# New estimates in a kernel builder's clock: program blocks, centring pieces, and the order that follows

## The chip, the cores and the metric

The kernel runs on one core of a Trainium2 chip. The metric is device time in microseconds; the time of a kernel is the median of several executions. One further execution is recorded by the hardware profiler, and all stages, gaps and rows below come from it. TensorE is called PE, VectorE DVE, ScalarE ACT, GpSimd POOL, and SyncE SP.

## The reference

Eight batches (B), eight heads (H), 576 positions (S), head size 64 (D): Nyström attention with 32 landmarks, and then a layer norm with two dense layers and a residual on the joined heads.

```python
q_lm = q.reshape(B, H, m, S // m, D).mean(axis=3)      # m = 32
k_lm = k.reshape(B, H, m, S // m, D).mean(axis=3)
A, Bm, C = sm(q, k_lm), sm(q_lm, k_lm), sm(q_lm, k)    # softmax of scaled products
Z = Bm.T / (norm1(Bm) * norminf(Bm) + 1e-06)
for _ in range(6):
    Z = 2 * Z - Z @ Bm @ Z
x = A @ Z @ C @ v                                      # heads joined: 8 x 576 x 512
xn = (x - mu) / np.sqrt(var + 1e-06) * g_ln
out = x + np.maximum(xn @ w_ch1, 0.0) @ w_ch2          # 512 -> 2048 -> 512
```

## The kernel before, in words

**The work.** Attention is done for batch 0, then 1, 2, the pair (3,4), the pair (5,6), and 7. A unit is four heads; a batch has two. `Coming` (L716) brings a set: `load` puts 576 KB of k, q or v into a ring of six staging tiles (SP's queue), `cast` (L775) makes fp16 of it on POOL (`nat`, or `natv` for v) and for some units also adds up the segments there (`asum`, `s`), `turn` and `turn_sums` or `add_up` transpose and sum on DVE (`xT`, `sT`, `part`), `spread` (L847) lays the landmarks out by a matmul and a copy on ACT (`lm`). `attention2` (L907) then has, in this order: the landmark scores, their softmax on DVE and `scores_k` (L864, exponentials `ec` on ACT, transposes `ecT` on DVE), `gram_of` (L663), six `iterate` (L683: a PE product, then one DVE operation that writes `st`), and beside them `scores_q` (L885, `ea`), the product with V in parts (`product`, L953, `pscv`), the divisors (`psd` on PE, two `lns` operations on ACT) and `normalize` (L509), which multiplies `ea` by `lns` on POOL. Last come `pszt`, `pszc`, the `zcbd` tiles (DVE), and `rows_of` (L697), which makes the attention's output block by block (`xblk`).

**The dense layers.** `First` (L1127) does a batch's first layer: four `product_of_heads` (L1135, "heads": eight matmuls, two copies to `m`), and sixteen chunks (L1158) of four matmuls into `psh`, each evacuated by a relu to `hT` on ACT or on DVE. `second_layer` (L1381) does the second in blocks of 128 rows, 16 matmuls a block; from batch 4 on most of it goes as seven half-size products (`seven_products`, L1312), for which POOL mixes W2 (`mix_w2`, L1267) and DVE mixes `hT`. W1 is centred in place by eight DVE operations of 1024 columns (`center_w1`, L1120), two for each quarter of the columns, after batch 1's last `product_of_heads`.

**What sets the order.** Nothing in the order of instructions is written out by hand for the middle of the kernel. The kernel's own builder keeps a clock (`Clock`, L83): each recorded operation goes through `note` (L146), which adds an estimated duration (`took`, L124) to the engine's time and notes when its tiles are ready and free. `run` (L1509) holds four streams (attentions, first layers, batch 0's rows, second layers). Each says from what time its next piece could go; the first that could go by now is taken, in that order of preference, and where none can, the soonest. Before each choice `help_out` (L1424) places stores, loads, POOL casts, centring pieces and DVE jobs, if the engine's estimated time is near enough. The instructions keep the order of recording on each engine. So an estimate changes no operation but may change every order.

The clock also counts matmuls, for the blocks in which PE's program is fetched: a `mark` at which the next block is taken to begin (L93), `BLOCK` matmuls later the next one (L103), and `fetched`, the estimated end of the running fetch: `FETCH` ns after the mark while loads are on the wire, 3000 otherwise (L178 to L181). At a mark the clock holds PE until `fetched`; `calm` (L105) lets attention's dense pieces of some 40 to 72 matmuls ask whether a mark comes inside them.

```python
        def calm(self, n):

            return self.fetched if self.count + n + (20 if late() else 0) >= self.mark else 0.0
```

Where there is nothing to do for PE, `warm` (L463) puts a matmul on zeros.

Of the kernel before, what the change touches and what calls it, by code (L numbers as in the profile page):

```python
# [20 lines left out]
def kernel(  # L21
# [19 lines left out]
    KCH = DM // P  # L41
    MCH = HID // P
# [19 lines left out]
    def name_of(x):  # L62
        return x.tensor.name if hasattr(x, "tensor") else x.name

    parted, mixed_ = {}, set()

    def key_of(ap):

# [2 lines left out]
    def keys_of(ap):  # L71
        n = name_of(ap)
        if n not in parted:
            return [n]
        at = [ap.offset]
        for step, k in list(ap.ap)[1:]:
            if step >= parted[n]:
                at = [o + step * i for o in at for i in range(k)]
        if n in mixed_:
            return [f"{n}:{o // parted[n]}:{int(o % parted[n] >= 256)}" for o in at]  # L80
        return [f"{n}:{o // parted[n]}" for o in at]

    class Clock:  # L83
# [5 lines left out]
        def __init__(self):  # L89
            self.free = dict.fromkeys(("PE", "DVE", "Activation", "Pool", "SP"), 0.0)  # L90
            self.wrote, self.used, self.begun = {}, {}, {}
            self.small, self.lanes, self.wire = False, {}, 0.0
            self.cells, self.count, self.mark, self.fetched = [], 0, 100, 0.0  # L93

        def share(self, span=3400.0):

# [3 lines left out]
        def now(self):  # L100
            return max([self.free["PE"]] + list(self.lanes.values()))

        BLOCK, FETCH = 127, 4300  # L103

        def calm(self, n):  # L105

# [17 lines left out]
        def took(self, i, e, n, m):  # L124
            op = type(i).__name__
            if e == "Activation":
                return 190 + 0.79 * n
            if e == "Pool":
                if n == 1024 and name_of(i.outs[0].bass_ap) in mixed_:
                    return 2080  # L130
                if "Ptr" in op:
                    return 100 + 1.29 * n
                return 100 + 0.92 * n if "Copy" in op else 280 + 1.76 * n
            if n == 1152 and "Copy" in op:
                return 760
            if "Stats" in op:
                return 690 if m > 100 else 180
            if n >= 512 and (n == 576 or op == 'InstTensorCopy'):
                return 100 + 1.13 * n
            if n == 1024:  # L140
                return 690 if name_of(i.outs[0].bass_ap) in mixed_ else 900
            if "Transpose" in op:
                return 110 + 1.15 * n
            return 140 + 1.15 * max(n, m if "Reduce" in op else 0)

        def note(self, i):  # L146
            e = str(i.engine).rsplit(".", 1)[-1]
            outs = [a.bass_ap for a in i.outs if hasattr(a, "bass_ap")]
            ins = [a.bass_ap for a in i.ins if hasattr(a, "bass_ap")]
            size = [[k for _, k in a.ap] for a in outs + ins]  # L150
            count = []
            for dims in size:
                n = 1
                for k in dims[1:]:
                    n *= k
                count.append(n)
            reads = [n for a in ins for n in keys_of(a)]
            writes = [n for a in outs for n in keys_of(a)]
            ready = 0.0
            for n in reads:  # L160
                t, who = self.wrote.get(n, (0.0, e))
                if who != e or e != "PE":
                    ready = max(ready, t + (self.WAY if who != e else 0.0))
            for n in writes:
                for t, who in (self.wrote.get(n, (0.0, e)), self.used.get(n, (0.0, e)),
                               (self.begun.get(n, 0.0), "")):
                    if who != e:
                        ready = max(ready, t + self.WAY)
            if type(i).__name__ == "InstDMACopy":
                start = max(self.free[e], ready)  # L170
                self.free[e] = start + (580 if e == "SP" else 100)
                self.wire = max(start + 1650, self.wire) + count[0] * size[0][0] * 4 / 385.0
                done = self.wire + 600 + min(2200, 0.6 * (self.wire - start - 1650))
                start = done
            elif e == "PE":
                cols = count[0]
                self.count += 1
                if self.count >= self.mark:  # L178
                    self.mark += self.BLOCK
                    ready = max(ready, self.fetched)  # L180
                    self.fetched = max(self.now(), ready) + (self.FETCH if self.wire > self.now() else 3000)  # L181
                rows_, cols_ = tuple(i.tile_size)
                self.cells.append((self.now(), cols / 2.4 * rows_ * cols_ / 128 ** 2))
                if tuple(i.tile_size) == (128, 128):
                    if self.small:
                        self.free[e] = max(list(self.lanes.values()) + [self.free[e]]) + 100
                        self.small, self.lanes = False, {}
                    start = max(self.free[e], ready)
                    self.free[e] = start + max(cols / 2.4 + 3, 56)
                    done = self.free[e] + 160  # L190
                else:
                    if not self.small:
                        self.small, self.lanes = True, {}
                        self.free[e] += 95
                    lane = [(a, c) for a in range(i.tile_position[0], i.tile_position[0] + rows_, 32)
                            for c in range(i.tile_position[1], i.tile_position[1] + cols_, 32)]
                    start = max([self.free[e], ready] + [self.lanes.get(x, 0.0) for x in lane])
                    self.lanes.update((x, start + max(cols / 2.4, 30)) for x in lane)
                    self.free[e] = start + (8 if rows_ == 64 and cols < 128 else 4)
                    done = self.lanes[lane[0]] + 160  # L200
            else:
                start = max(self.free[e], ready)
                done = start + self.took(i, e, count[0], max(count[1:] + [0]))
                self.free[e] = done - self.OVERLAP[e]
            for n in reads:
                self.used[n] = max(self.used.get(n, (0.0, e)), (done, e))
            for n in writes:
                self.wrote[n] = max(self.wrote.get(n, (0.0, e)), (done, e))
# [160 lines left out]
    w1_16 = wpool.tile([P, KCH, HID], FP16, name="w1_16")  # L369
    w2_16 = wpool.tile([P, MCH, DM], FP16, name="w2_16")  # L370
    parted[w1_16.name] = parted[w2_16.name] = 512
    w1_src = moe_w_ch1.rearrange("(c p) f -> p c f", p=P)
    w2_src = moe_w_ch2.rearrange("(m p) d -> p m d", p=P)
    xpool = Ring(name="xpool", bufs=12)
# [137 lines left out]
    heads, ready, multiplied, cast_v = {}, set(), {0}, {0}  # L512
# [1094 lines left out]
```

## Time and profile before

| what | value |
|---|---|
| median of 3 runs | 286.38 us |
| lowest and highest | 285.69, 287.48 us |
| the profiled execution | 287.15 us |
| its span on the core | 285.4 us |
| granted PE clock, mean | 1.000 |
| PE, DVE, ACT, POOL busy | 267.0, 216.0, 162.5, 159.2 us |
| HBM read and written | 36.70 and 9.44 MB |

The span runs from the first to the last instruction; 1.75 us of the profiled execution lie around it. Busy times overlap, since the engines run side by side; what counts is the engine that ends a wait last. A timeline row has a start and a length in us, the engine, the tiles written and read, their shapes, and in brackets the idle time before it with what ended it. "issue" there means that the profile shows nothing that the engine waited for.

How the stages lie in the span, by the order of PE's matmuls and their times in the trace: batch 0's attention to 24 us, batch 1's from 43 to 54, batch 2's from 73 to 89, the pair (3,4) from 110 to 133, batch 3's first layer from 133 to 152, batch 4's from 152 to 168, the pair (5,6) from 139 to 180, batch 5's first layer from 188, batch 7's attention from 225 to 237, batch 7's first layer from 244 to 258, and second layers to the end.

### The profile page before, as it was taken

Reading aid. Unit: us, or ns where it says so; the run is one execution under the profiler, and the core shown is the slowest. Engines: PE = TensorE matmul, PEld = TensorE weight load, DVE = VectorE, ACT = ScalarE, POOL = GpSimd, SP = SyncE. Lnnn points to the kernel's source line nnn. Section 1 sums busy time; section 2 is a strip of 40 time slices with the busy share of each in tenths; the row PEclk is TensorE's granted clock in tenths of the full one; section 3 lists DMA queues with packets and bytes.
Section 4 is the critical chain, followed back from the end, with each engine's and each line's share of the span. In section 5 each row is a group of like instructions: output and inputs, shape, how many; then the busy total and the mean of one; then the engine's idle time right before and its main releaser. Section 6 shows DMA issues by size and latency. Waiting matters only on the chain.

```text
span 285.4 us, 8685 instructions
## 1 busy us (share of the span) xinstructions
PE 267.0 (94%) x3620; PEld 165.5 (58%) x3620; DVE 216.0 (76%) x480; ACT 162.5 (57%) x286; POOL 159.2 (56%) x187
## 2 busy tenths in 40 slices
PE   7887999998899899989889999999999999999994
PEld 7644554345334465434455555467876766678883
DVE  3558985999999754998798842899697299747761
ACT  2566955278633787336999866647338653672000
POOL 5377777999999999998999975610000030100000
PEclk9999999999999999999999999999999999999999
DMA  7999999987744589792830011130041004300606
GB/s 246 386 390 386 385 390 393 310 274 252 246 122 133 192 272 329 216 315 56 261 112 2 2 34 44 39 74 2 0 111 41 0 5 99 89 0 2 147 19 167
DMA packets 23375, 46.70 MB, mean 164 GB/s; under 512 B 2212, under 2 KB 2472, under 8 KB 23336
## 3 DMA queue, kind: packets, MB, share of 16 engines
q1 hardware_dynamic: 23176, 46.02, 49.9%
q8 instruction: 28, 0.46, 0.6%
q10 hardware_dynamic: 160, 0.13, 0.2%
q14 instruction: 11, 0.09, 0.1%
HBM read 36.70 MB, written 9.44 MB: 162 GB/s over the span
## 4 chain that ended last, share of the span: by engine, by line
PE 47%; POOL 18%; DVE 14%; DMA 13%; issue 4%; ACT 1%; SPq 1%; POOLq 0%; DVEq 0%; ACTq 0%
PE bank L272 31%; PE psh L272 13%; POOL natv L266 6%; DMA stg<-in_v_dram 6%; DMA wstg<-in_moe_w_ch_dram 5%; POOL asum L266 4%; POOL nat L266 4%; DVE w L266 3%; DVE xblk L266 2%; DVE xT L266 2%; DMA stg<-in_k_dram 2%; POOL ea L266 2%; DVE part L266 1%; DVE m L266 1%; DVE six L266 1%
## 5 line engine op out<-in xcount | busy, mean ns | idle before, releaser
L272 PE MATMUL bank<-w,hT 128*128 128x512 f16 (+1 forms) x528 | 108.7, 335 | 1.4 <-issue 1.4
L266 ACT ACTIVATE hT<-psh 128x576 f16<-128x576 f32 x114 | 71.3, 651 | 18.5 <-PE psh L272 16.6
L272 PE MATMUL psh<-ea,m 128*128 128x288 f16 x512 | 77.4, 286 | 3.1 <-ACT hT L266 1.3
L272 PEld LDWEIGHTS <-hT 128*128 128x128 f16 x656 | 60.6, 98 | 32.7 <-issue 7.1
L272 PEld LDWEIGHTS <-m 128*128 128x128 f16 x512 | 47.9, 97 | 24.8 <-issue 10.0
L266 DVE SCALAR_TENSOR_TENSOR xblk<-bank,rstd,xblk 128x256 f32<-128x256 f32 (+1 forms) x77 | 39.2, 541 | 24.6 <-PE bank L272 24.5
L266 POOL TENSOR_TENSOR ea<-ea,lns 128x576 f16<-128x576 f16 x14 | 18.1, 1305 | 47.9 <-ACT lns L266 47.9
L266 POOL CAST natv<-stg 64x1152 f16<-64x1152 f32 (+1 forms) x23 | 26.7, 1159 | 12.5 <-DMA stg<-in_v_dram 8.7
L266 POOL CAST nat<-stg 128x1152 f16<-128x1152 f32 x28 | 32.5, 1177 | 2.0 <-DMA stg<-in_k_dram 1.1
L266 ACT CAST m<-bank 128x512 f16<-128x512 f32 x31 | 17.5, 587 | 12.9 <-PE bank L272 12.7
L266 ACT COPY xblk<-bank 128x512 f32<-128x512 f32 (+1 forms) x32 | 17.8, 589 | 11.9 <-PE bank L272 11.8
L266 DVE BATCH_NORM_STATS2 six<-xblk 128x6 f32<-128x512 f32 x36 | 24.3, 674 | 0.3 <-ACT xblk L266 0.2
L266 DVE STREAM_TRANSPOSE xT<-nat 128x576 uint32<-128x576 uint32 x28 | 21.5, 767 | 1.1 <-POOL nat L266 0.8
L266 DVE TENSOR_REDUCE part<-xT 128x32 f16<-128x576 f16 x28 | 20.3, 743 | 0.3
L266 ACT ACTIVATE lns<-psd 128x576 f32<-128x576 f32 x16 | 10.3, 646 | 17.1 <-PE psd L272 17.1
L266 POOL TENSOR_TENSOR asum<-asum 128x256 f32<-128x256 f32 (+1 forms) x28 | 17.5, 626 | 2.2
L266 DVE CAST m<-bank 128x512 f16<-128x512 f32 x17 | 11.7, 687 | 7.6 <-PE bank L272 7.4
L266 POOL TENSOR_TENSOR asum<-nat 128x512 f32<-128x512 f16 x14 | 16.8, 1200 | 1.1
L272 PE MATMUL bank<-w2mix,hT 128*128 128x256 f16 x128 | 16.5, 273 | 0.0
L272 PE MATMUL bank<-w2mix 128*128 128x256 f16 x128 | 16.0, 273 | 0.0
L272 PE MATMUL bank<-zcbd,ea 128*128 128x256 f16 (+1 forms) x80 | 13.9, 275 | 1.5 <-DVE m L266 0.8
L272 PE MATMUL bank<-w,zt 64*32 64x512 f16 x256 | 14.2, 386 | 0.5 <-ACT less L266 0.4
(123 smaller groups left out, 341.0 us busy)
## 6 DMA issues: line engine op xcount, KB each, us to landing
stg<-in_q_dram SPq DMA_DIRECT2D x16, 576.0 KB, 6.0
stg<-in_k_dram SPq DMA_DIRECT2D x16, 576.0 KB, 5.4
stg<-in_v_dram SPq DMA_DIRECT2D x16, 576.0 KB, 6.5
out_dram<-xblk SPq DMA_DIRECT2D x70, 128.0 KB, 2.3
wstg<-in_moe_w_ch_dram SPq DMA_DIRECT2D x16, 512.0 KB, 7.0
out_dram<-xblk ACTq DMA_DIRECT2D x2, 64.0 KB, 2.3
out_dram<-xblk SPq DMA_DIRECT2D x2, 64.0 KB, 2.0
g_rows<-in_moe_g_ln_dram SPq DMA_DIRECT2D x1, 2.0 KB
```

Source lines behind the costliest of these rows:

```text
L266: return lambda *args, **kw: keep(getattr(self.engine, op)(*args, **kw))
L272: keep(nc.tensor.matmul(o, l, r, start=start, stop=stop, tile_position=(rb, cb), skip_group_check=(skip or cb != 0)))
```

## The change

Four places in the clock get other numbers, and one rule is new. The first mark is at 116 matmuls instead of 100. A fetch is taken to last 5000 ns with loads on the wire instead of 4300, and 3300 without instead of 3000. A DVE operation of 1024 columns outside the mixing of `hT` (a centring piece of W1) is taken to last 1080 ns instead of 900. And when such a piece is recorded on a part of W1, POOL's estimated time moves on by 430 ns, counted from the piece's start if POOL would be free before.

```diff
-            self.cells, self.count, self.mark, self.fetched = [], 0, 100, 0.0
+            self.cells, self.count, self.mark, self.fetched = [], 0, 116, 0.0
...
-        BLOCK, FETCH = 127, 4300
+        BLOCK, FETCH = 127, 5000
...
-                return 690 if name_of(i.outs[0].bass_ap) in mixed_ else 900
+                return 690 if name_of(i.outs[0].bass_ap) in mixed_ else 1080
...
-                    self.fetched = max(self.now(), ready) + (self.FETCH if self.wire > self.now() else 3000)
+                    self.fetched = max(self.now(), ready) + (self.FETCH if self.wire > self.now() else 3300)
...
                 self.free[e] = done - self.OVERLAP[e]
+                if e == 'DVE' and count[0] == 1024 and writes[0] in parted_w1:
+                    self.free['Pool'] = max(self.free['Pool'], start) + 430
...
     parted[w1_16.name] = parted[w2_16.name] = 512
+    parted_w1.update(f"{w1_16.name}:{i}" for i in range(KCH * MCH))
```

None of these lines issues an instruction. The built program has 3618 matmuls on PE instead of 3620 (two matmuls on zeros fewer), and the same loads, casts, products and stores in another order, beginning with batch 1's attention. On DVE and ACT one evacuation changes engine.

More of the change, by code (lines that the diff above doesn't have):

```diff
@@ L63, in name_of @@
         return x.tensor.name if hasattr(x, "tensor") else x.name
-    parted, mixed_ = {}, set()
+    parted, mixed_, parted_w1 = {}, set(), set()
     def key_of(ap):
```

## The prediction

> **What bounds the kernel now.** First the page's engine totals and slices: which engine is full, and where.
>
> ```profile
> PE 267.0 (94%) x3620; PEld 165.5 (58%) x3620; DVE 216.0 (76%) x480; ACT 162.5 (57%) x286; POOL 159.2 (56%) x187
> ...
> POOL 5377777999999999998999975610000030100000
> PEclk9999999999999999999999999999999999999999
> DMA  7999999987744589792830011130041004300606
> ```
>
> The span has to hold TensorE's work. PE has 18.4 us of idle time in it; POOL is full from about 50 to 142 us; the clock is granted throughout, so no step below is a matter of clock. Next the stages, as busy time in windows (us of the window, then PE, PEld, DVE, ACT, POOL, clock, DMA share, GB/s).
>
> ```profile
> 95.00:110.00 15.00, 13.67 (x138) 8.21 (x144) 8.32 (x17) 11.54 (x22) 14.23 (x15) 1.00 0.72 235
> 110.00:126.00 16.00, 15.42 (x444) 7.40 (x427) 14.20 (x36) 8.22 (x13) 15.00 (x19) 1.00 0.87 280
> 126.00:141.00 15.00, 12.42 (x155) 6.06 (x153) 12.61 (x25) 10.04 (x20) 13.20 (x13) 1.00 0.54 159
> 141.00:152.00 11.00, 9.89 (x85) 5.92 (x84) 10.15 (x20) 10.28 (x18) 10.30 (x14) 1.00 0.36 126
> 152.00:168.00 16.00, 16.00 (x275) 9.31 (x275) 10.47 (x27) 13.44 (x25) 16.00 (x15) 1.00 0.01 2
> 168.00:188.00 20.00, 19.85 (x333) 9.75 (x331) 13.02 (x28) 11.32 (x21) 10.34 (x10) 1.00 0.23 53
> 188.00:285.00 97.00, 93.05 (x1034) 71.19 (x1026) 69.53 (x152) 42.46 (x77) 5.01 (x4) 1.00 0.23 53
> ```
>
> From 152 us on PE is full but for the tail; an order can only win before that. So third, PE's timeline around its gaps there (start, us, tile, idle before, releaser).
>
> ```profile
> 75.98 0.19 PE L272 MATMUL bank<-st,bones 128*128 128x64 f16 x1 [1.13 <-DVE st L266]
> ...
> 99.10 0.38 PE L272 MATMUL bank<-part,spread 128*128 128x256 f16 x2 [1.33 <-DVE part L266]
> ...
> 117.93 0.32 PE L272 MATMUL psea<-xT,lm 32*32 32x288 f16 x8 [0.56 <-issue]
> ...
> 127.85 1.90 PE L272 MATMUL bank<-w,hT 128*128 128x512 f16 x8 [1.38 <-issue]
> ...
> 141.15 1.07 PE L272 MATMUL psh<-ea,m 128*128 128x288 f16 x6 [0.70 <-ACT ec L266]
> ```
>
> Two gaps wait for DVE, two for nothing the profile names, one for ACT. The two unnamed ones are waits for program. The trace's DMA records show 28 instruction packets of 16,384 bytes on queue q8; one starts at 115.74 and PE resumes 2.2 us later, one at 125.44 and PE resumes 2.4 us later; the resumed matmuls are numbers 1503 and 1759 (from 0), 256 apart, so a block is 128 matmuls and edges lie at 95+128k. After both waits the next packet starts 1.63 us on, which is the fetch's free lead: an unhindered fetch costs 1.63 + 2.2 = 3.8 us. Counting from where the sequencer asks (it runs some 28 matmuls ahead: in the long stages packets start 1.63 us after number edge-28), these two took about 7 us, with the DMA share at 0.87.
>
> Last, the queues behind those gaps.
>
> ```profile
> 70.03 5.30 DVE L266 TENSOR_TENSOR w<-w,less 128x1024 f16<-128x1024 f16 x5
> ...
> 131.54 2.61 POOL L266 TENSOR_TENSOR ea<-ea,lns 128x576 f16<-128x576 f16 x2 [1.27 <-ACT lns L266]
> ...
> 140.28 1.48 ACT L266 ACTIVATE ec<-psec 128x576 f16<-128x576 f32 x2
> 141.83 2.71 ACT L266 ACTIVATE hT<-psh 128x576 f16<-128x576 f32 x4
> ```
>
> **The change part by part.** No operation is added and only two PE fillers of 0.28 us at most go; six estimates of the builder change, and the order follows. I compared the two programs' orders engine by engine; matmul numbers are places in PE's order. Up to number 609 PE's order is the same. Then A(n) is the attention of batch n.
>
> *A(1), number 610.* The product with V is put after one more iteration and two second-layer matmuls. It waited 0.42 us for natv; POOL casts k1 ahead of both ea, filling its 0.59 us wait there and making ea 0.5 us later, which nobody needs before 57 us. Gain 0 to 0.4 at PE, counted 0, since first layer 1 that follows is paced by evacuation.
>
> *Centring.* A piece costs 0.93 us at the median, one 1.62. The old estimate 0.9 put five ahead of A(2)'s softmax, the new 1.08 puts four. Softmax's row sum starts 1.62-0.08 us earlier, the gap of 1.13 shrinks to about 0.2: gain 0.9. The piece returns behind the transposes of ec; there nine second-layer matmuls (9x0.215=1.9 us) now stand in front of the first iteration and cover it. Each later iteration still queues on DVE behind a transpose (0.77) or a sum (0.74); I give 0.2 back. Net -0.7.
>
> *The 430 ns on POOL.* It moves no work. [...] I take 0.
>
> *spread for (3,4), second half.* It moves from number 1216 to 1264, behind 48 matmuls (some 4 us). It waited for DVE's part at 99.05, which waited for POOL's sum at 98.45; PE now gets there after 101. Gain 1.3. On SP, loads of (3,4) v2, v3 and (5,6) k0, k1 now stand behind stores of blocks that DVE finishes at 82 to 95 us; casts need them at 102 to 107, so nothing is late.
>
> *Fetches.* Three more second-layer matmuls (0.65 us) stand before edge 1503: its gap of 0.56 goes, gain 0.5. Between edges 1631 and 1759, 5 such matmuls stand instead of 11: 1.3 us less cover. If the fetch takes 3.8 us there is no gap, if 7 about 2.5; the nearest row is the same block's old fetch, under nearly the same loads, so I take a gap of 1.5 for 1.38: +0.1. [...]
>
> *POOL's ea of A(3,4)* move ahead of the cast and sums of (5,6) q3 (1.14+1.16+1.26+0.42 = 3.9 us). Start about 123 instead of 127.74. They may wait for lns behind the fetch, so q3's cast and sums end near 135 and natv near 142.4, 1 us later. DVE's sum of q3 stands ahead of b3's second m copy and would hold it, but DVE gets there only at 135.7. Cost 0, up to 1 if POOL slips more; PE keeps its lead. Loads q3 and v1 wait behind stores on SP until 108 and 115; needed at 131 and 136.
>
> *A(5,6), the largest move.* Its first scores_k leave the stretch before b3's first layer for b4's; the second scores_k, gram and all six iterations leave b4's first layer for b3's second. At 139.44 to 141.15 that frees 1.71 us (scores 0.73, filler 0.28, wait 0.70) and ACT's 1.48 us. The stage behind it is ACT's (10.28 of 11): 13 relus x0.68 + 4 copies x0.53 = 11.0; after it has 12 and 3, 9.8, one of each on DVE, which loses transposes (the second lm copy, 0.5, only changes places with m1's wait). Gain 1.7+1.0 = 2.7. Paid back later: 0.73 of scores on full PE. Net -2.0.
>
> *Iterations in b3's second layer.* Matmul time is the same. Between iterations stand 2 to 5 long matmuls plus scores or product: 0.9 to 2.1 us per step, 6.6 over five; a step costs at least 1.04 (old A(5,6), last step) and in A(3,4) averaged 1.77, 8.9 over five. The loss is 0 to 2.3. Edges 2271 and 2399 come about 4.2 us after one another for a 3.8 us fetch in quiet DMA (0.01 to 0.23): 0 to 1. I take 1.3 together. POOL takes natv for (7) ahead of ea(5,6); batch 5's product is done early enough.
>
> *From 188 us* the content and nearly the whole order are the same: 0, bounds -0.3 to +1.
>
> Sum: -0.7-1.3-0.5+0.1-2.0+1.3 = -3.1 us. The profiled execution took 287.15 (span 285.4 and 1.75 around it), so 284.1; the median shown is 0.77 lower, 286.38, which gives 283.3 us.
>
> **The rivals.** *Absorbed* (same): gains ahead of 142 us are eaten because POOL, without rest to 142, sets when (3,4) and (5,6) can go, so leads made on PE turn into waits. For it: POOL's row of nines, and 18% of the chain. Against it: PE's waits for POOL's products are short (0.4 for ea). Then only the A(5,6) net stays less 1.3: 286.38-0.7 = 285.7.
>
> [...]
>
> *Late fetches in a row* (slower): new order packs small matmuls closer, so a fetch under load costs 7 us three times running, at 1503, 1631 and 1759. Asked on resuming at 115.2 the next lands at 122.2 (PE there at 119.7: 2.5), the next at 129.2 (125.5 needed: 3.7). That is 4.7 more than forecast; with 2.0 each at 2271 and 2399 less my 1.0, 283.3+4.7+3.0 = 291.0. It decides once these waits pass 3.1+2.9 = 6 us. For it: 7 us was seen twice; against: the fetch between them took 3.8, and DMA is quiet after 144.
>
> **How the numbers follow.** Forecast 0.58, absorbed 0.22, late fetches 0.20. The forecast's own range is 281.3 to 284.8 (terms at their ends: -2.0 for a shorter b3 stage and no waits, +1.5). One per cent, 2.9 us, is about what a measurement of this kernel can tell from no change; faster starts at 283.5. Of the forecast 0.47 is faster and 0.11 same; of absorbed 0.03, 0.14 and, with a wait more than I see, 0.05 slower; of late fetches 0.02 same and 0.18 slower. Faster 0.50, same 0.27, slower 0.23. Range 281.0 to 289.5.
>
> **What would show it.** Right: the gap before bank<-st,bones under 0.4; none before part,spread; no issue gap near 117; b3's relus taking under 10.2 us with no ec before them; b5's heads (187.8 us in the profile before) about 3 us sooner. Wrong: issue gaps of over 2 us, PE waiting for st in b3's second layer by more than 2 us in sum, or ea(3,4) finishing after 133.

## The result and the profile after

The changed kernel takes 281.95 us, the median of 6 executions (281.32 to 284.31), against 286.47 us for six of the kernel before (285.69 to 287.70): a ratio of 0.985, 95% interval 0.981 to 0.989. The forecast was 283.3 us. The profiled execution took 282.81 us (span 281.0), 4.34 less than that of before.

On the page of the changed kernel first the engine totals, the slices of POOL and the clock, then the first line of the chain that ended last.

```profile
PE 266.2 (95%) x3618; PEld 165.6 (59%) x3618; DVE 212.3 (76%) x479; ACT 161.9 (58%) x287; POOL 160.1 (57%) x187
...
POOL 5368778999999999978999999310000040100000
PEclk9999999999999999999999999999999999999998
...
PE 79%; DVE 9%; ACT 5%; issue 3%; DMA 2%; SPq 0%; DVEq 0%; ACTq 0%
```

The same line of the kernel before:

```profile
PE 47%; POOL 18%; DVE 14%; DMA 13%; issue 4%; ACT 1%; SPq 1%; POOLq 0%; DVEq 0%; ACTq 0%
```

PE has 0.8 us less to do and VectorE 3.7, POOL 0.9 more; that is not where 4.3 us come from. What changed is the chain. Before, 45 per cent of it ran through POOL, VectorE and DMA; now 79 per cent is PE's own work. The changed kernel's timeline of PE in (3,4)'s attention and batch 3's first layer (start, length, tiles, idle time before and what ended it):

```profile
115.19 0.32 PE L274 MATMUL psea<-xT,lm 32*32 32x288 f16 x8 [1.20 <-issue]
...
119.74 0.29 PE L274 MATMUL bank<-st 32*32 32x64 f16 x15 [0.49 <-issue]
...
124.02 1.46 PE L274 MATMUL bank<-w,hT 128*128 128x512 f16 x6 [0.99 <-issue]
...
142.48 1.14 PE L274 MATMUL psh<-ea,m 128*128 128x288 f16 x8 [0.36 <-DVE hT L268]
```

These are the largest that are left from 70 us on. The two waits for VectorE (1.13 at A(2)'s gram, 1.33 at the spread) and the one for `ec` (0.70) are gone; the waits for program are not: the one at matmul 1503 has grown from 0.56 to 1.20, one of 0.49 has come at 1631, and that at 1759 went from 1.38 to 0.99.

VectorE's timeline shows how the first two went: four pieces stand ahead of the softmax, and the sums of q3 (`sT<-s`) stand behind the four row measures (`six`, `stats`) of batch 2.

```profile
69.35 3.49 DVE L268 TENSOR_TENSOR w<-w,less 128x1024 f16<-128x1024 f16 x4
72.78 0.22 DVE L268 TENSOR_REDUCE rsum<-bank 128x2 f32<-128x64 f32 x1
...
98.98 0.66 DVE L268 BATCH_NORM_STATS2 six<-xblk 128x6 f32<-128x512 f32 x1
99.68 0.18 DVE L268 BATCH_NORM_AGGREGATE stats<-six 128x2 f32<-128x6 f32 x1
99.78 0.21 DVE L268 STREAM_TRANSPOSE sT<-s 128x64 uint32<-128x64 uint32 x1
```

Two stages of the changed kernel as windows, with the columns of the windows before: batch 3's first layer from its second chunk on, and batch 4's.

```profile
134.86:145.83 10.97, 9.63 (x86) 5.99 (x78) 10.28 (x24) 9.51 (x18) 10.48 (x10) 1.00 0.78 231
145.83:159.97 14.14, 14.14 (x160) 8.29 (x160) 8.88 (x14) 12.32 (x23) 13.63 (x16) 1.00 0.01 2
```

Batch 3's stage takes 10.97 us for 10.79 in the kernel before: it has not become shorter, though ACT has less in it (9.51 us for 10.13).

**A ledger.** Kernels with different orders can't be compared at equal times. So for each group of matmuls the shortest time that it took in either kernel is added up in PE's order, and subtracted from the time at which PE really was there. The difference between two kernels is then the lead at equal work done. The first seven columns below are the lead over the kernel before in us (minus is sooner) at: the begin of batch 1's second layer (so far nothing differs that could count; it is what executions differ by at their start), A(2)'s last product, batch 2's third head product, the begin of A(3,4), the begin of batch 3's rows, the end of batch 4's first layer, and the end; then the waits that PE's timeline shows from 70 us on, by what ended them, and the time lost to a reduced clock, (1 - mean clock) x span. All are of the profiled executions, one for each kernel; that of e2 is the fastest of its ten (285.06 us, median 287.66), so its row shows more than its ratio below.

| kernel | b1 layer 2 | A(2) | b2 heads | A(3,4) | b3 rows | b4 end | end | VectorE | ACT | issue | clock |
|---|---|---|---|---|---|---|---|---|---|---|---|
| before | 0 | 0 | 0 | 0 | 0 | 0 | 0 | 3.71 | 1.80 | 1.94 | 0 |
| after | -0.48 | -2.73 | -4.19 | -4.02 | -3.65 | -5.67 | -4.23 | 1.04 | 0.95 | 2.68 | 0.84 |
| e1 | 0.29 | -1.71 | -3.17 | -2.74 | -2.55 | -2.41 | -2.41 | 1.04 | 2.20 | 2.48 | 0 |
| e2 | -0.63 | -0.67 | -1.90 | -1.52 | -2.94 | -4.06 | -2.31 | 3.30 | 0.83 | 1.45 | 0.57 |
| e3 | -0.23 | -1.11 | -2.60 | -2.55 | -4.27 | -4.59 | -4.60 | 1.37 | 2.00 | 0.43 | 0 |
| e4 | -0.46 | -0.47 | -0.46 | -0.46 | -0.44 | -1.93 | 0.53 | 3.79 | 2.75 | 1.96 | 0 |
| e5 | 1.12 | -1.12 | -2.58 | -2.40 | -3.73 | -3.83 | -3.84 | 0.85 | 3.19 | 0 | 1.69 |
| e6 | 1.35 | 0.04 | -1.42 | -1.42 | -2.79 | -4.82 | -3.34 | 1.74 | 1.11 | 1.07 | 0 |
| e7 | -0.02 | -2.27 | -3.73 | -3.53 | -4.84 | -6.86 | -5.30 | 1.06 | 2.06 | 0 | 0 |
| e8 | -0.08 | -0.06 | -1.52 | -0.15 | 2.89 | 2.90 | 2.89 | 3.52 | 2.05 | 3.30 | 2.30 |
| e9 | -0.29 | -1.63 | 0.22 | 1.85 | 0.47 | 1.42 | 1.42 | 4.68 | 2.41 | 0.79 | 1.72 |
| e10 | -0.23 | -1.57 | -1.46 | -0.26 | -1.52 | -1.20 | -0.95 | 4.51 | 2.19 | 0.57 | 1.14 |
| e11 | -0.09 | -1.10 | -2.59 | -2.54 | -4.33 | -6.36 | -4.91 | 1.77 | 0.95 | 0.71 | 0 |
| e12 | 0.04 | -1.32 | -2.78 | -2.74 | -1.23 | -3.39 | -0.92 | 1.70 | 4.05 | 0 | 1.99 |

Read along the row of after: of 4.23 us, 0.48 is the start, 2.25 is made in A(2), 1.46 up to batch 2's third head product, 0.54 is lost again up to batch 3's rows, 2.02 is made up to the end of batch 4's first layer and 1.44 of it paid back behind. The 0.84 us of reduced clock in this row costs nothing: it lies in the last 2 us of the span, where PE has no work left (the window 279.00:281.00 has a clock of 0.54 and 0.00 us of PE). e1 to e12 are the experiments.

### The profile page after: what moved, and what is told of

Its sections match the earlier page's. It is cut to its first block, busy times and chain, and to the rows that moved or that the text cites. A ratio compares the mean times of both kernels' runs of the same rounds, so it can differ in the third digit from the quotient of the medians.

```text
span 281.0 us, 8678 instructions
## 1 busy us (share of the span) xinstructions
PE 266.2 (95%) x3618; PEld 165.6 (59%) x3618; DVE 212.3 (76%) x479; ACT 161.9 (58%) x287; POOL 160.1 (57%) x187
## 4 chain that ended last, share of the span: by engine, by line
PE 79%; DVE 9%; ACT 5%; issue 3%; DMA 2%; SPq 0%; DVEq 0%; ACTq 0%
PE bank L274 51%; PE psh L274 21%; DMA stg<-in_q_dram 2%; ACT hT L268 2%; DVE xblk L268 2%; PE pscv L274 2%; DVE m L268 2%; DVE xT L268 1%; PE psec L274 1%; PE psd L274 1%; DVE part L268 1%; ACT ec L268 1%; DVE hT L268 1%; ACT lns L268 1%; PE psea L274 1%
## 5 line engine op out<-in xcount | busy, mean ns | idle before, releaser
L268 ACT COPY xblk<-bank 128x512 f32<-128x512 f32 (+1 forms) x34 | 19.1, 588 | 12.2 <-PE bank L274 12.0
L268 DVE SCALAR_TENSOR_TENSOR st<-st,bank 128x128 f16<-128x128 f16 (+2 forms) x36 | 11.1, 308 | 6.4 <-PE bank L274 6.0
```

The source lines that it names most:

```text
L268: return lambda *args, **kw: keep(getattr(self.engine, op)(*args, **kw))
```

## The experiments

Each ratio is to executions of the kernel before made beside the experiment, whose medians were 287.19 to 288.09 us; experiments are to be compared by these ratios, not by their times.

### Which part carries the gain (e1 to e4)

e1 is the kernel before with the new estimate of a centring piece and nothing else:

```diff
-                return 690 if name_of(i.outs[0].bass_ap) in mixed_ else 900
+                return 690 if name_of(i.outs[0].bass_ap) in mixed_ else 1080
```

> Only the centring estimate (1080) is new. In the built order four pieces stand ahead of A(2)'s softmax, spread for (3,4) comes six chunks later and ea(3,4) ahead of q3's cast, while A(5,6) begins before b3's first layer as in the kernel before. Theory of the early stages (the time came from A(2) and the spread, A(5,6)'s move being worth 0.5 net): the gaps before bank<-st,bones and before part,spread are gone, about 284.1 us. Rival (A(5,6)'s move is the gain): about 286.

Measured: 284.39 us, ratio 0.986 (0.981 to 0.991). This one number puts four pieces ahead of A(2)'s softmax and the second half of (3,4)'s spread behind chunk 9, while A(5,6) stays in its old place. It brings nine tenths of the change's gain, and the two intervals overlap.

e2 is the kernel before with only the first mark changed:

```diff
-            self.cells, self.count, self.mark, self.fetched = [], 0, 100, 0.0
+            self.cells, self.count, self.mark, self.fetched = [], 0, 116, 0.0
```

> Only the first mark (116) is new. A(2) has its scores_q later, but five pieces stay ahead of its softmax; A(5,6) moves as in the changed kernel. Theory of the early stages: the gap before bank<-st,bones stays near 1.1, so the time falls by about 1, to 285.4 us. Rival (A(5,6)'s move is the gain): 283.5.

Measured: 287.66 us, ratio 0.996 (0.991 to 1.001): A(5,6) is late here, five pieces stand ahead of the softmax, and little is gained. VectorE still waits 0.88 us for POOL at the sums of q3.

e3 is the changed kernel with the estimate of a piece put back to 900 ns:

```diff
-                return 690 if name_of(i.outs[0].bass_ap) in mixed_ else 1080
+                return 690 if name_of(i.outs[0].bass_ap) in mixed_ else 900
```

> The changed kernel with the old centring estimate (900). A(1) and A(2)'s scores_q move as in the changed kernel, spread too, but five pieces stay ahead of A(2)'s softmax and A(5,6) begins before b3's first layer. Theory of the early stages: 0.4 from A(1), 1 from A(2), 1 from the spread, about 284.1 us. Rival (A(5,6)'s move is the gain): about 286.

Measured: 283.71 us, ratio 0.983 (0.977 to 0.988). Five pieces are back ahead of the softmax, A(5,6) is in its old place, and nothing is lost against the changed kernel. So neither the four pieces instead of five nor the late A(5,6) is needed for the gain.

e4 is the kernel before with A(5,6) held until batch 3's first layer is done, all else as it was:

```diff
-            yield lambda: max(0.0 if mine else banks.next(), ps2.next("p2", 2), clock.calm(64), aexp.next("e", 4),
-                              clock.at(c.lm_tile[y], *[xT["k", w] for w in pair]))
+            yield lambda: NEVER if bs == (5, 6) and 3 not in first_done else max(
+                0.0 if mine else banks.next(), ps2.next("p2", 2), clock.calm(64), aexp.next("e", 4),
+                clock.at(c.lm_tile[y], *[xT["k", w] for w in pair]))
```

> The kernel before with A(5,6) alone held back until b3's first layer is recorded; the order is that of the kernel before up to matmul 1862. Theory of the early stages: the wait at b3's chunk m1 goes, but scores and iterations are paid back in full stages, 0 to 1 us faster, about 286.0 us. Rival (A(5,6)'s move is the gain): 283.5.

Measured: 288.61 us, ratio 1.002 (0.998 to 1.005). The ledger shows both halves: 1.49 us made from batch 3's rows to the end of batch 4's first layer, 2.46 paid back behind. The largest term of the forecast, by itself, is worth nothing that the interval shows.

### The late attention undone, the program blocks, the loads (e5 to e7)

e5 is the changed kernel in which batch 3's second chunk waits for A(5,6) to have begun, so that A(5,6) is early again:

```diff
+            if bs == (5, 6):
+                begun56.append(y)
...
-            yield lambda: max(ps2.next("p2"), clock.at(l1.m16[m // 4], *l1.ea))
+            yield lambda: (NEVER if b == 3 and m == 1 and not begun56 else
+                           max(ps2.next("p2"), clock.at(l1.m16[m // 4], *l1.ea)))
```

> The changed kernel with b3's chunk m1 held until A(5,6)'s first scores_k are recorded, so that these, gram and the iterations stand where the kernel before had them; the order is the changed kernel's up to matmul 1860. Theory of the early stages: 0.5 us over the changed kernel's 282, up to 1.5 with a wait for POOL's sums of q3 (133.9 us), so 282.5 to 283.5. Rival (A(5,6)'s move is the gain): 285 or more.

Measured: 284.51 us, ratio 0.987 (0.980 to 0.995). The wait for `ec` is back (0.59), the stages behind pay nothing back (-3.83 at batch 4's end, -3.84 at the end), and the time is the changed kernel's within the intervals. Something else in this run matters below: its PE shows no wait for "issue" at all, though up to batch 3's rows it has the changed kernel's order and its loads.

e6 is the changed kernel with 18 more matmuls on zeros at the very start, which moves all block edges by 18 places against the work and leaves the order as it was:

```diff
-            warm(3, 256)
+            n0 = clock.count
+            warm(*((12, 64) if (w, nm) != (1, "q") else (3, 256)))
+            clock.count = n0 + 3
```

> The changed kernel with two times three fillers of 256 columns at the start cut into twelve of 64, 18 matmuls more; all else keeps its order. Block edges then fall 18 matmuls earlier in the work. If the issue gaps are waits for a program block, they move from content numbers 1503, 1631 and 1759 to 1485, 1613 and 1741, the first ahead of nearly all of scores_q for (5,6)'s forerunner (3,4). If they are waits for data, they stay before the same matmuls. Time within 0.7 us of the changed kernel either way, about 282.

Measured: 283.24 us, ratio 0.984 (0.978 to 0.991). The timeline of PE in this kernel, waits for "issue" only:

```profile
119.16 0.26 PE L274 MATMUL bank<-st 32*32 32x64 f16 x10 [0.70 <-issue]
123.98 0.28 PE L274 MATMUL psd<-ea,bones 128*128 128x288 f16 x1 [0.37 <-issue]
```

Without the 18 these are matmuls 1613 and 1741, each 18 places before a gap of the changed kernel (1631 and 1759). These two gaps moved with the edges and not with the work, so they are waits for program blocks. The third, at 1503, has no counterpart at 1485: e6 shows no wait there.

e7 is the changed kernel with loads of batches 5 and 6 of one ninth the size; the casts repeat the ninth, so that every engine has the same instructions to run:

```diff
+        part = slice(0, 1 if b in (5, 6) else NJ)
...
-            out=t[:],
+            out=t[:, :, part, :],
...
-            pool.tensor_copy(out=t[:], in_=stg[:])
+            pool.tensor_copy(out=t[:], in_=stg[:, :, 0:1, :].broadcast_to([P, 2, NJ, D])
+                             if b in (5, 6) else stg[:])
```

> The changed kernel with a ninth of the bytes in each load of (5,6): one position of nine is loaded and POOL's casts repeat it, so the output for batches 5 and 6 is not the reference's; the order is the same on all engines. Loads of (5,6) run from about 95 to 125 us. If the fetches are late because of loads on the DMA engines, the packet that starts 4.7 us after its free lead at 112.7 comes early, and the issue gaps of 1.2, 0.7 and 1.2 us before 1503, 1631 and 1759 shrink to under 0.3 each: 279 to 280 us. If a fetch is late whatever else runs, or POOL sets the pace there, the time stays near 282.

Measured: 281.60 us, ratio 0.980 (0.974 to 0.987). No wait for "issue" is left in A(3,4). At its last product the ledger shows a lead of 6.09 us, where the changed kernel has about 3.65: 2.4 us more (2.9 with the start's 0.46 taken off). But 1.25 of it goes at once to a new wait, 0.92 us for `lns` on ACT, with smaller ones:

```profile
126.71 0.25 PE L275 MATMUL pszc<-cv,st 32*32 32x64 f16 x16 [0.92 <-ACT lns L269]
```

That loads make the gaps does not follow from this run alone, since e5 has none either with its loads in full, and the interval of e7 overlaps that of the changed kernel. The DMA records of all the kernels speak for it. Take A(3,4)'s first program packet, the one for edge 1503, and its free lead as the prediction estimates it: it should start 1.63 us after matmul 1347. (Counted in this way, the 13 packets from 149 us on start 0.98 to 3.00 us after their matmul in the kernel before, 1.76 at the median, and 1.15 to 2.99 in the changed one, 1.94 at the median; so up to 1.37 us late is seen there too.) From 2 to 4 us after that matmul the DMA share is 0.45 in e7 and 0.35 in e9, whose PE comes there later than in any other kernel, and the packet starts 1.02 and 0.69 us late. In the other twelve kernels the share is 0.89 to 1.07, and it starts 2.00 to 4.69 us late. So the packets start later where more is loaded, but by how much differs between executions with the same order and loads (4.69 us in the changed kernel, 2.45 in e5), and in e5 the delay was covered. The 2.4 us are thus the difference of two executions, not a fixed price of the loads.

### A theory that fell (e8 to e10)

By then the gain seemed to be made by two separate moves in the early stages: the fifth piece behind A(2)'s softmax, and the spread's second half at chunk 9. Each was put alone into the kernel before, and then both. e8:

```diff
-                yield lambda: c.spread_ready(y)
+                yield lambda: (NEVER if c.bs == (3, 4) and y == 1 and chunks2[0] < 9 else c.spread_ready(y))
```

> The kernel before, with the second half of (3,4)'s spread held until chunk 9 of batch 2's first layer (matmul 1264, where the changed kernel has it, instead of 1216); orders before it are unchanged, five W1 pieces still go ahead of A(2)'s softmax, and A(5,6) stays where it was. Theory (the gain is made in the early stages, in two separate parts): level with before until A(2)'s last product, 1.3 to 1.5 us ahead by batch 2's third head product, the gap before the spread gone; total 1.0 to 1.5 us less, ratio about 0.995. Rival 1 (the spread's wait only moves to the next stage): 0 to 0.3 us. Rival 2 (the spread is worth more than the piece and carries the whole change): 3 us or more.

Measured: 289.58 us, ratio 1.005 (1.001 to 1.009). The lead of 1.5 us is there at batch 2's third head product, as expected, and gone again when A(3,4) begins. PE's timeline of e8:

```profile
101.64 1.14 PE L272 MATMUL psh<-ea,m 128*128 128x288 f16 x8 [1.24 <-DVE hT L266]
...
128.72 2.69 PE L272 MATMUL bank<-w,hT 128*128 128x512 f16 x8 [2.47 <-issue]
```

The wait of 1.33 us for `part` has come back as one of 1.24 us for a relu, that of chunk 5. VectorE's timeline of e8 shows why:

```profile
98.11 0.25 DVE L266 STREAM_TRANSPOSE sT<-s 128x64 uint32<-128x64 uint32 x1 [0.92 <-POOL s L266]
...
100.86 0.72 DVE L266 TENSOR_SCALAR hT<-psh 128x576 f16<-128x576 f32 x1
```

`sT<-s`, VectorE's part of q3's sums, stands still 0.92 us for POOL, and everything behind it in VectorE's queue, the relu of chunk 5 too, is late. Freeing PE of the wait did not free VectorE of it. The rest of e8's loss is a wait for a program block of 2.47 us (1.38 before) and a reduced clock (0.92, 0.50 and 0.72 in the windows of 2 us from 128 us on, below).

e9 holds VectorE's side work after the fourth piece until A(2)'s softmax is out (`laid` counts pieces, `soft2` is filled by the softmax):

```diff
-            if clock.free["DVE"] <= now + lead():
+            if clock.free["DVE"] <= now + lead() and (len(laid) != 4 or soft2):
```

> The kernel before, with the fifth W1 centring piece held until A(2)'s softmax has been issued; the second half of (3,4)'s spread stays at chunk 3 of batch 2's first layer (before the early place that costs 1.4 us), A(5,6) stays where it was. Theory: what counts is the 1.62 us that the fifth piece takes ahead of the softmax beside GpSimd's work, so 1.6 to 2.3 us ahead at A(2)'s last product; total 1.3 to 2.0 us less, ratio about 0.994. As the prediction had it (0.9 us of gain, 0.2 paid back): 0.7 us, ratio 0.9975. Rival (the iterations absorb it, their bound being VectorE's queue): 0 to 0.3 us.

Measured: 289.08 us, ratio 1.006 (1.003 to 1.008). A(2) is ahead by 1.63 us, 1.34 without the start, and batch 2's first layer takes all of it and more, with two waits on PE:

```profile
96.91 0.65 PE L272 MATMUL psh<-ea,m 128*128 128x288 f16 x4 [1.43 <-DVE hT L266]
...
99.13 0.39 PE L272 MATMUL bank<-part,spread 128*128 128x256 f16 x2 [1.57 <-DVE part L266]
```

e10 has both holds.

> Both holds together on the kernel before: fifth piece behind A(2)'s softmax, second half of (3,4)'s spread at chunk 9 of batch 2's first layer; the builder's own estimates, its fetch estimate and the place of A(5,6) unchanged. Theory: the two gains add, 2.6 to 3.5 us, ratio about 0.989, the larger part of the change without any of its estimates. Rival (they take from the same slack, since both end in A(3,4)): no more than the larger of the two alone, about 2 us, ratio 0.993.

Measured: 286.49 us, ratio 0.997 (0.995 to 1.000). The gains did not add; 0.26 us of lead is left when A(3,4) begins. Again PE waits for VectorE, and VectorE for POOL; PE's timeline of e10, then VectorE's:

```profile
96.60 1.14 PE L272 MATMUL psh<-ea,m 128*128 128x288 f16 x8 [1.43 <-DVE hT L266]
...
101.03 0.54 PE L272 MATMUL psh<-ea,m 128*128 128x288 f16 x3 [0.58 <-DVE m L266]
```

```profile
94.03 0.25 DVE L266 STREAM_TRANSPOSE sT<-s 128x64 uint32<-128x64 uint32 x1 [1.04 <-POOL s L266]
...
95.82 0.72 DVE L266 TENSOR_SCALAR hT<-psh 128x576 f16<-128x576 f32 x1
98.20 0.25 DVE L266 STREAM_TRANSPOSE sT<-s 128x64 uint32<-128x64 uint32 x1 [1.66 <-POOL s L266]
```

### An attempt at a better estimate, and the missing move (e11, e12)

e11 is the changed kernel with e3's 900 ns and e9's hold, an attempt at a faster one.

> The changed kernel with the estimate of a W1 piece put back from 1080 to 900 ns and the fifth piece held until A(2)'s softmax has been issued. Its gram is then behind no piece, the second half of (3,4)'s spread stands after batch 2's last head product, and A(5,6) is as late as in the changed kernel. Theory: A(2) is at least as far ahead as in the changed kernel (2.3 us), perhaps 0.7 us more since no piece stands ahead of the gram; the rest as there; total 280.5 to 282, ratio 0.980 to 0.985. Rival (the stages behind pay the extra back): ratio as the changed kernel's, 0.985, or a little above.

Measured: 283.22 us, ratio 0.985 (0.982 to 0.988), the changed kernel's ratio; the rival's case. A(2) is less far ahead (-1.01 without the start, for -2.25); PE waits 0.51 us for `cv` there, which with one piece fewer ahead of the gram now stands behind the last ones.

e12 adds to e10 what the changed kernel has on VectorE in batch 2's first layer: the sums of q2 and q3 later in its queue.

```diff
+                if self.bs == (3, 4) and (nm == "q" and w == 2 and chunks2[0] < 2
+                                          or nm == "q" and w == 3 and blocks_done.get(2) != 4):
+                    return NEVER
                 return clock.at(self.sums[i])
```

> The kernel with both holds (fifth piece behind A(2)'s softmax, second half of (3,4)'s spread not before chunk 9), and besides it VectorE's additions of GpSimd's sums for (3,4): those of q2 not before chunk 2 of batch 2's first layer, those of q3 not before batch 2's four rows are measured, which is where the changed kernel has them. A(5,6) then begins as late as in the changed kernel (matmul 1964). New theory (the two early gains are lost in batch 2's first layer as long as VectorE's queue has these additions, which wait for GpSimd, ahead of relus): none of the waits for hT or m behind VectorE of 1.43, 0.58 and 0.29 us that the kernel with both holds had there, 2.8 to 3.3 us ahead of before when A(3,4) begins (that kernel: 0.3 us), and 2.0 to 4.0 us less in all, ratio 0.986 to 0.993, the width being the waits for program blocks in A(3,4). Rival 1 (the lead is lost to GpSimd itself, which reaches its last cast for (3,4) at the same time whatever VectorE does): 0.3 to 1 us ahead when A(3,4) begins, ratio 0.997. Rival 2 (what is gained goes to longer waits for program blocks): ahead by 3 us at A(3,4)'s begin and by under 1 us at its end.

Measured: 285.76 us, ratio 0.996 (0.993 to 1.000). The new theory was right for the place that it speaks of: the three waits for VectorE are gone, and A(3,4) begins 2.74 us ahead where e10 had 0.26 (2.8 to 3.3 expected, so just short). It was wrong in all: 1.4 us for the 2.0 to 4.0 expected, and no wait for a program block to blame. PE now comes to A(3,4)'s end too early. Its timeline in e12, then ACT's:

```profile
125.23 0.30 PE L272 MATMUL pszt<-st,cv 32*64 32x32 f16 x16 [1.28 <-ACT lns L266]
126.48 0.31 PE L272 MATMUL pszc<-cv,st 32*32 32x64 f16 x16 [0.95 <-ACT lns L266]
126.72 1.46 PE L272 MATMUL bank<-w,hT 128*128 128x512 f16 x3
```

```profile
124.53 0.65 ACT L266 ACTIVATE lns<-psd 128x576 f32<-128x576 f32 x1 [2.13 <-POOL ea L266]
```

ACT's third `lns` waits 2.13 us for POOL, which still has q2's cast and sums and only then multiplies the first `ea`; PE waits for ACT, and then has a granted clock of 0.57 and 0.58 in the windows 126 to 128 and 128 to 130 us. From a lead of 4.99 us at the last divisor, 1.23 is left at batch 3's rows. In the changed kernel POOL is no sooner there (122.79 us for 123.21). Its builder has put more second-layer matmuls between the last divisor and these products (7 for 4), which covers part of the wait, but not all of it: in e7 (line above) and e5, which have the changed kernel's order there and no wait for program, PE waits 0.92 and 0.90 us for `lns` at this place. In the changed kernel's own profiled execution PE came late enough, after 2.68 us of waits for program. Which of the new estimates puts the 7 matmuls there was not tested.

## Why the forecast held, and where it was wrong

The forecast was -3.1 us on the profiled execution, measured were -4.34; direction and range were right, but the steps did not all hold: the one on A(2) was mis-sized by a factor of three, the one on fetches failed, and one taken as 0 hides a condition on which the gain is kept. The sum came near because the errors partly cancel: A(2) gave 1.55 us more than forecast and the start 0.48, A(3,4) with its fetches 0.77 less, and the rest differs by 0.17 or less a step. By its steps, with the ledger (the prediction speaks of six estimates; five numbers change):

- *A(1), number 610*: taken as 0. The 0.48 us in the ledger is no gain of it: e4, which has the old order there, has 0.46.
- *Centring*: taken as -0.7, measured -2.25. The step had "gain 0.9" at the gram and "I give 0.2 back" in the iterations. The gram gained 1.30 (the gap of 1.13 went altogether), and the iterations gained 0.95 more where the step expected a loss. e1 has the same two parts, 1.29 and 0.71. The second part does not come from the four pieces: e9, e10 and e12 have four as well, and gain 1.2 at the gram but under 0.2 in the iterations, while e3 with five gains 0.6 there. It goes with the number of pieces on VectorE between the `st` of the gram and that of the first iteration, one in the changed kernel, e1 and e3, two in the kernel before, e2, e9, e10 and e12. VectorE's timeline of the changed kernel, then of e9, shows these pieces:

```profile
76.12 0.68 DVE L268 TENSOR_TENSOR w<-w,less 128x1024 f16<-128x1024 f16 x1
```

```profile
76.17 2.07 DVE L266 TENSOR_TENSOR w<-w,less 128x1024 f16<-128x1024 f16 x2
```

So the step saw the first part and under-sized it, and missed the second: where the later pieces go.

- *The 430 ns on POOL*: taken as 0 because "it moves no work". Beside the eight pieces of the kernel before, eight POOL rows are 0.32 to 0.46 us longer than their twins elsewhere (1.05 for 0.72, 1.60 for 1.15, ...), 2.9 us in all; in the changed kernel they are 3.1 us longer, so this did not become less. But an estimate also places work. In e8 to e10, with the builder's old picture of POOL and VectorE, the sums that wait for POOL stand ahead of relus in VectorE's queue, and the gains of 1.5 and 1.3 us are lost by the begin of A(3,4). The kernels that have the 430 ns or the 1080 ns but not both, e3 and e11 (430) and e1 (1080), keep theirs. In the table the waits for VectorE are 3.3 to 4.7 us in every kernel with neither (before, e2, e4, e8, e9, e10) and 0.85 to 1.77 in all others; among these e12 has neither estimate, but its holds put the sums where the mended clock puts them. That this order keeps the lead up to A(3,4) is shown by e12 against e10 (2.74 us for 0.26). That the 430 ns make the order in e3 and e11 is argued, since both also have the new mark and fetch times. And e2 is an exception: with neither number, and with 3.30 us of waits for VectorE, its profiled execution keeps most of what it gained.
- *spread for (3,4), second half*: taken as -1.3, measured -1.46. Right in size; but whether the lead stays depends on the order of the sums in VectorE's queue (e8, e12).
- *Fetches*: taken as -0.4, measured with the rest of A(3,4) as +0.37 (from its begin to batch 3's rows), and as waits for "issue" 2.68 us for 1.94. "Its gap of 0.56 goes, gain 0.5" failed: PE reached that edge sooner, the packet started 4.69 us late instead of 3.49 in the kernel before, and 0.65 us more cover was not enough, so the gap grew to 1.20. The gap at 1759 was near the estimate (0.99 for 1.5). e6 shows what these gaps are; e5 shows that the order alone does not fix their size: in the same order they came to 0 in one execution and to 2.68 us in the other. The rival *late fetches in a row* came in part: three such waits, but of 1.20, 0.49 and 0.99 us, 2.68 in all, not the 6 us from which it decides.
- *POOL's ea ahead of q3*: taken as 0, up to 1. `ea` is done at 129.80 us for 134.15, with no wait shown for it, so 0 stands. What it would cost now to have q3 first again was not tried.
- *A(5,6) and the iterations behind*: taken as -2.0 + 1.3 = -0.7, measured -2.02 + 1.44 = -0.58. The sum was right, and so were both halves, the first one partly by luck. Inside the first one, "1.0" from a shorter stage was wrong (10.97 us for 10.79); instead of it the second layer beside batch 4's first gained 0.49, and the rest came ahead of batch 3's second chunk, where the wait of 0.70 us for `ec` is gone. What is paid back is not waits for `st` but many pauses of under 0.3 us around the iterations; the only one long enough for a row is 0.19. e4 shows how little this term is bound to be a gain.
- *From 188 us*: 0, measured 0 from batch 6 on.

Of the signs it named, the gaps at A(2)'s gram and at the spread are gone, and batch 5's heads come at 182.98 us for 187.80, 4.8 sooner instead of 3. Two signs of being right did not come: the gap near 117 is still there (1.20 us, at 115.19), and batch 3's relus take 10.97 us and not under 10.2. None of the signs of being wrong came.

The rival *absorbed* said that gains ahead of 142 us turn into waits because POOL sets the pace. It did not carry the changed kernel's time, but it happened to four of the experiments (e8, e9, e10, e12), through a queue in which something that waits for POOL stood ahead of something for PE, and it shows in the changed kernel's own order as soon as the waits for program are away (0.90 us in e5, 0.92 in e7). The forecast gave it 22 in 100; its argument against, that PE's own waits for POOL are short, looked at PE alone and not at VectorE and ACT.

What stays open: how much of the kept lead is due to the 430 ns, since of the new numbers only the 1080 ns and the mark were run alone; and what the new fetch times do, which were never run alone. That e12 pays back 2.47 us behind batch 4 where the changed kernel pays 1.44 is one wait: PE waits 1.07 us for `zt` on ACT at 184.37 us, and e4 shows the same one.

## What to carry to other kernels

When a scheduler's estimate is mended, don't price the moves that it makes one by one: a wait taken from PE by a move made by hand came back within a stage in e8, e9 and e10, because the queue of the engine that PE waits for still had the late operation in front, and when that was moved too (e12), most of the lead went one stage later to the next engine that waits for POOL. Ask of each removed wait which engine was late, what stands behind the late operation on that engine's queue, and whether the estimate that placed it is mended too. And compare kernels by their lead at equal work, stage by stage: it shows gains that are lost again, which two totals can't.

## What the runs showed of the hardware

**Half clock after a gap.** In e8, behind the wait of 2.47 us, five matmuls that elsewhere take 1.24 us take 1.95. The windows of e8 from 128 us on (the column before the last two is the granted clock):

```profile
128.00:130.00 2.00, 1.28 (x6) 0.58 (x7) 1.23 (x2) 0.00 (x0) 1.96 (x2) 0.92 0.42 119
130.00:132.00 2.00, 2.00 (x7) 0.84 (x6) 0.98 (x2) 0.01 (x1) 0.00 (x0) 0.50 0.00 0
132.00:134.00 2.00, 2.00 (x9) 0.92 (x8) 1.93 (x6) 1.35 (x3) 0.57 (x1) 0.72 0.49 113
```

The 0.50 of the middle window is taken as the only reduced rate (the clock records in the traces of before and after hold 1.0 and 0.5 and nothing else). By this estimate a window of 2 us that shows 0.92 has 0.32 us of it, and 0.72 has 1.12: together 0.32 + 2.00 + 1.12 = 3.44 us at half clock, a loss of 1.7 us on top of the gap. In e12, after waits of 1.28 and 0.95 us, the windows show 0.57 and 0.58 for 4 us, which is 3.40 us in the same way. In e9, after waits of 1.43 and 1.57 us with 0.65 us of matmuls between, they show 0.51 and 0.64 for 4 us, again 3.40; four matmuls into `psh` take 1.14 us there (at 100.48 us) and 0.65 at 109.89 us. Single gaps of 1.20 us (the changed kernel), 1.38 (before) and 1.78 (e1) left the clock at 1.00. So the wait of 2.47 us for a program block and the half clock behind it cost PE 4.2 us together. What a single gap between 1.78 and 2.47 us does was not measured.

**Program blocks under loads.** The waits for "issue" in A(3,4) lie 128 matmuls apart (1503, 1631 and 1759 in the changed kernel), and e6, with 18 matmuls more ahead, has two of them 18 places earlier in the work. From the first of these edges to the second PE takes 4.55 us in the changed kernel and to the third 4.28 more, and the fetch is not always hidden: up to 2.47 us of gap at one edge (e8). Where the DMA share was 0.35 and 0.45 (e9, e7), the first packet there started 0.69 and 1.02 us late; where it was 0.89 to 1.07, 2.00 to 4.69 us late. With the loads cut to a ninth no gap was left (e7), but e5 has none either, with the order and loads of the changed kernel, which has 2.68 us.

**VectorE and POOL side by side.** The eight centring pieces are the same operation, but in the kernel before and the changed one they take 0.66 to 1.21 us, and at their longest 1.62 and 1.63. In the kernel before, the two longest run beside POOL's casts of 128x1152, which take 1.60 us there for 1.15 elsewhere. Such a piece was the fifth ahead of the softmax, which is why one piece cost as much as it did.
